# A chunked-attention and mixture-of-experts kernel: input loads in 2 KB runs four tiles ahead, v's loads tied to the next round's turns, and a routing table cleared in two steps

## The chip, the cores and the metric

The kernel runs on one core of a Trainium2 chip. The metric is the device time of one execution, in microseconds, lower is better. A profile of one execution shows what each engine did: PE (TensorE, matmuls), PEld (its weight loads), DVE (VectorE), ACT (ScalarE), POOL (GpSimd) and SP (SyncE, which here only issues DMAs). Sixteen DMA engines move all data between memory and the core, whoever issues the transfer.

## What is computed

Attention inside chunks of 64 tokens, then a mixture of experts that sends each token to one of eight experts:

```
# q, k, v: [8, 8, 576, 64] float32
scores = q_c @ k_c.T / 8 per chunk of 64;  attn = softmax(scores);  out = attn @ v_c
x = out.transpose(0, 2, 1, 3).reshape(4608, 512)
logits = x @ w_gate + modality_bias[modality_id]        # [4608, 8]
e_idx = argmax(logits);  gate_w = softmax(logits)[e_idx]
for e in range(8):                                      # w1[e]: 512x1024, w2[e]: 1024x512
    out[e_idx == e] = gate_w * (relu(x[e_idx == e] @ w1[e]) @ w2[e])
```

## The kernel before

The 4608 tokens are 36 tiles of 128. For each tile the attention stage does the following. `scores` (L248) multiplies q by k in 64 by 64 blocks, eight heads by two chunks; DVE takes the maximum and subtracts it (L250, L252); `exps` has ACT take the exponential (L257) and POOL add the two halves of each row (L258); `sums` has DVE finish the sum (L262). `transposes` (L269) turns the exponentials on PE and ACT copies them out (`at`, L271). `values` (L282) multiplies them by v, again in 64 by 64 blocks, and ACT copies the result out (`xt`, L285). `rows` (L294) multiplies with an identity beside the gate's weights, which gives the tile's rows and its logits; DVE scales them (`xr`, L296); `put` has ACT store the logits (L306) and issue the store of the rows to memory (`xd`, L307).

The order is written out by hand (`manual_schedule`) in rounds of four tiles (`ROUNDS`; the first three rounds have one, one and two tiles). A round k that begins with tile a has two halves. In the first half, the turns, PE does `transposes` of tiles a to a+3 and `rows` of the four tiles before. In the second half PE alternates `scores` of the next round's tiles with `values` of this round's. So 64 by 64 matmuls, with very many instructions for PE, fill the second half, and matmuls of the whole array the first. The PSUM tiles `ap` (of `transposes`) and `xp` (of `values`) share a ring of two buffers; ACT's copies `at` and `xt` free them.

The loads of q and k (`load_qk`, L116, 512 KB a tile, one tile `qk`) and of v (`load_v`, L122, 256 KB) are issued on SP's queue, which is in order; each waits until its buffer is free. Six buffers of each stand in a ring: behind `scores(t)` comes the load of q and k for tile t+6, behind `values(t)` the load of v for tile t+6.

Routing starts before attention is over. The tokens are routed in two groups, the first 14 tiles and the other 22 (`GROUPS`). `route` finds each token's expert and its row in a table in memory, `tab`, of 8 experts by 4608 rows of 64 bytes. `scatter` (L384) has POOL write one row for each token, an indirect DMA for each tile, 14 in the first group. Rows that no token took must hold an index out of bounds, so the table is cleared ahead: POOL fills a buffer with that value, and `clear_part` (L191) issues three DMAs of 768 KB on ACT's queue, one in round 5 and two in round 6 (`CLEARS`), each after the round's turns. After the first group, `locate` (L522) has SP read the first three slots' lists of tokens from the table (`tl`), POOL copies the indices (`tk`, L539), and `gather` (L543) has POOL fetch the rows of the slot's 384 tokens from `xd` into `xg`, in three indirect DMAs. `split` then turns these rows on PE (`tp`, L583), and the expert stage begins: 384 tokens a slot, for each of eight slices `first` (L640) and `second` (L653), every product in three passes of high and low parts. `fetch` (L600) has SP load the weights, and ACT and DVE split them (L611, L615).

What the program's builder orders by itself: DMAs issued from SP and ACT take turns on eight completion semaphores, DMAHW0 to DMAHW7, and POOL's indirect DMAs on eight others, DMASW0 to DMASW7. An access to `tab` whose rows are found at run time counts as one to the whole table; only the scatters are declared free of each other.

Of the kernel before, what the change touches and what calls it, by code (L numbers as in the profile page):

```python
# [8 lines left out]
F32 = mybir.dt.float32  # L9
# [10 lines left out]
P = 128  # L20
N = B * S
DM = H * D
E = 8
# [3 lines left out]
NT = N // P  # L27
NP = H // 2
SLOT = 384
# [5 lines left out]
BUSY = 4  # L35
SIZES = (1, 1, 2) + 8 * (4,)
ROUNDS = [(sum(SIZES[:i]), n) for i, n in enumerate(SIZES)]
CLEARS = (5, 6, 6)
PLAN = {
    -10: {"fetch": [(0, 1)]},  # L40
    -9: {"fetch": [(1, 1)]},
# [25 lines left out]
CAP = N  # L67
ROW = 16
# [4 lines left out]
NEG = 1  # L73
GMAX = max(n for _, n in GROUPS)
OFF = 16
EARLY = sum(n for _, n in GROUPS[:NEG])
# [18 lines left out]
def attention_moe(ctx: ExitStack, tc: tile.TileContext, qkv, mod, cst, bias, wcat, wfst, out):  # L95
    nc = tc.nc
    V, A, PE, G, SP = nc.vector, nc.scalar, nc.tensor, nc.gpsimd, nc.sync

    cp = ctx.enter_context(tc.tile_pool(name="cp", bufs=1))
    wk = ctx.enter_context(tc.tile_pool(name="wk", bufs=2))  # L100
# [6 lines left out]
    tab = dr.tile([E * CAP, ROW], I32, name="tab")  # L107


    NB = 6  # L110
    st = {}

    def load_qk(t):
        if t < NT:
            b = wk.tile([P, 2, DM], F32, name="qk", bufs=NB)
            SP.dma_start(b, qkv[t][:, 0:2])  # L116
            st[t] = {"qk": b}

    def load_v(t):
        if t < NT:  # L120
            b = wk.tile([P, DM], F32, name="v", bufs=NB)
            SP.dma_start(b, qkv[t][:, 2])  # L122
            st[t]["v"] = b

    cs = cp.tile([P, C_END], F32, name="cs")
# [5 lines left out]
    consts(C_I, C_GW)  # L131
    load_qk(1)
    load_v(0)
    load_qk(2)
    load_v(1)
    load_qk(3)
    load_v(2)
    load_qk(4)
    load_v(3)
    load_qk(5)  # L140
    load_v(4)
    load_v(5)
    bs = cp.tile([P, 2, E], F32, name="bs")
    mid = cp.tile([P, 2 * NT], I32, name="mid")

# [7 lines left out]
    ident = cs[:, C_I:C_I + P]  # L153
# [24 lines left out]
    tid = cp.tile([P, NT], I32, name="tid")  # L178
    G.iota(tid, pattern=[[P, NT]], base=0, channel_multiplier=1)
    oob = rawr[2].bitcast(I32)  # L180
    nclear = 3
    wclear = ROW * E * CAP // P // nclear
    oob = oob.rearrange("p a b -> p (a b)")[:, 0:wclear]
    G.memset(oob, OOB)
    tabp = tab.rearrange("(p a) c -> p (a c)", p=P)
    clears = []

    def clear_part():
        i = len(clears)
        if i < nclear:  # L190
            clears.append(A.dma_start(tabp[:, i * wclear:(i + 1) * wclear], oob))  # L191

    SYNC = mybir.DependencyInfo(mybir.DependencyClass.Sync, mybir.DependencyReason.DATA)

    def after(inst, names):
        for n in names:
            tc.add_manual_dep(inst.ins, n, SYNC, reason="rows of the token table")

    def apart(inst, key):
        tc.declare_no_dep(inst.ins, group=key, reason="scatters to different rows")  # L200
        tc.add_to_no_dep_group(key, inst.ins)
# [63 lines left out]
    def transposes(t):  # L265
        ex = st[t]["ex"].rearrange("p h k -> p (h k)")
        ap = ps.tile([P, NP, P], F32, tag="t", name="ap")
        for p in range(NP):
            PE.transpose(ap[:, p, :], ex[:, p * P:p * P + P], ident)  # L269
        at = mp.tile([P, DM], F32, tag="yo", name="at", bufs=4).rearrange("p (a c) -> p a c", a=NP)  # L270
        A.copy(at, ap)  # L271
        st[t]["at"] = at

    def values(t):
        v, at = st[t]["v"], st[t]["at"]
        xp = ps.tile([P, NP, P], F32, tag="t", name="xp")
        for p in range(NP):
            for c in range(2):
                vs = slice(p * P + c * 64, p * P + c * 64 + 64)
                for hh in range(2):  # L280
                    hs = slice(hh * 64, hh * 64 + 64)
                    PE.matmul(xp[hs, p, c * 64:c * 64 + 64], v[hs, vs],  # L282
                              at[hs, p, c * 64:c * 64 + 64], start=True, stop=True)
        xt = mp.tile([P, DM], F32R, tag="h", name="xt", bufs=6).bitcast(F32).rearrange("p (a c) -> p a c", a=NP)
        A.copy(xt, xp)  # L285
        st[t]["xt"] = xt
# [92 lines left out]
        pooljobs.append(scatter(g, pi, tg))  # L379

    def scatter(g, pi, tg):
        assert len(clears) == nclear
        for j in range(GROUPS[g][1]):
            w = G.indirect_dma_start(  # L384
                tab, bass.IndirectOffsetOnAxis(ap=pi[:, j:j + 1], axis=0),
                tg[:, j, :], None, bounds_check=E * CAP - 1, oob_is_err=True)
            after(w, [c.ins.name for c in clears])
            apart(w, "tab")
            marks.append(w.ins.name)
            yield  # L390
# [342 lines left out]
    scores(0)  # L733
    load_qk(NB)
    exps(0)
    late_consts()
    scores(1)
    load_qk(NB + 1)
    busy(BUSY)

    done, scored = 0, 2
    for k, (a, n) in enumerate(ROUNDS):
        whole = range(done, a) if k > 1 else ()
        for j in range(max(n, len(whole))):
            if j < n:
                transposes(a + j)
                if not k:
                    exps(1)
            if j < len(whole):
                rows(whole[j])  # L750
            if j < n:
                sums(a + j)
            if j < len(whole):
                put(whole[j])
                done = whole[j] + 1
                for g, (t0, m) in enumerate(GROUPS):
                    if t0 + m == done:
                        jobs.append(route(g))
            advance(None if j % 2 else [pooljobs])
        if k == 2:  # L760
            prepare()
        for _ in range(CLEARS.count(k)):
            clear_part()
        upto = a + 3 if k < 2 else a + n + ROUNDS[k + 1][1] if k + 1 < len(ROUNDS) else scored
        small = range(scored, upto)
        scored = upto
        for j in range(max(n, len(small))):
            if j < len(small):
                scores(small[j])
                load_qk(small[j] + NB)  # L770
            if j < n:
                values(a + j)
                load_v(a + j + NB)
            if j < len(small):
                exps(small[j])
            advance()
            if j < n:
                plan(a + j - NT)
# [26 lines left out]
def _pack(inputs):  # L805
    import numpy as np

    def chunks(a):
        return a.reshape(B, H, S // 64, 64, D).transpose(0, 2, 1, 3, 4).reshape(NT, 2, H, 64, D)

    q, k, v = (chunks(np.asarray(inputs[n])) for n in ("q", "k", "v"))
    qt = q.transpose(0, 1, 4, 2, 3).reshape(NT, 2, 64, DM)
    kt = k.transpose(0, 1, 4, 2, 3).reshape(NT, 2, 64, DM)
    vv = v.reshape(NT, 2, NP, 2, 64, D).transpose(0, 3, 4, 2, 1, 5).reshape(NT, 2, 64, DM)
    qkv = np.stack([qt, kt, vv], axis=3).reshape(NT, P, 3, DM)

    wg = np.asarray(inputs["moe_w_gate"])
    c = np.zeros((P, C_END), np.float32)
    gw = c[:, C_GW:C_GW + NP * GWC].reshape(P, NP, GWC)
    gw[:, :, 0:P] = np.eye(P, dtype=np.float32)[:, None, :]  # L820
    for hh in range(2):
        gw[hh * 64:(hh + 1) * 64, :, P + hh * E:P + (hh + 1) * E] = \
            wg.reshape(NP, 2, 64, E)[:, hh].transpose(1, 0, 2)
    c[:, C_GW:C_GW + NP * GWC] = gw.reshape(P, -1)
    c[:, C_I:C_I + P] = np.eye(P, dtype=np.float32)
    c[:, C_U:C_U + P] = np.triu(np.ones((P, P), np.float32), 1)
    c[:, C_REV:C_REV + E] = np.arange(E, 0, -1)
    c[:, C_CAP:C_CAP + E] = np.arange(E) * CAP
    c[:, C_EID:C_EID + E] = np.arange(E)
    c[:, C_DE:C_DE + 2 * E] = np.diff(np.arange(2 * E) % E, prepend=0)  # L830
    c[:, C_THR:C_THR + 3 * NJ] = (np.arange(NJ) * SLOT + np.arange(3)[:, None] * P).reshape(-1)
    c[:, C_LOW:C_LOW + 4 * E * E] = np.tril(np.ones((2 * E, 2 * E), np.float32), -1).reshape(-1)
    c[:, C_SID:C_SID + NREST] = np.arange(NREST)
    c[:, C_STP:C_STP + E], c[:, C_STP + E:C_STP + 2 * E] = SLOT, TAIL
    c[:, C_PEN + TAIL // P:C_PEN + NTT] = OOB
    c[:, C_TH2:C_TH2 + NJ2] = np.arange(NJ2) * TAIL

    w1 = np.asarray(inputs["moe_w1"]).reshape(E, NK, P, NF, P).transpose(0, 2, 3, 1, 4).reshape(E, P, NF, DM)
    w2 = np.asarray(inputs["moe_w2"]).reshape(E, NF, P, DM).transpose(0, 2, 1, 3)
    wcat = np.concatenate([w1, w2], axis=3)  # L840

    w1 = np.asarray(inputs["moe_w1"]).reshape(E, NK, NJB, 32, NF, P).transpose(0, 1, 3, 4, 2, 5).reshape(E, P, NF, DM)
    wfst = np.concatenate([w1, w2], axis=3)
    mod = np.ascontiguousarray(np.asarray(inputs["moe_modality_id"]).astype(np.int64).reshape(NT, P).T)
    bias = np.ascontiguousarray(np.broadcast_to(np.asarray(inputs["moe_modality_bias"])[None], (P, 2, E)))
    return {"qkv": qkv, "mod": mod, "cst": c, "bias": bias, "wcat": np.ascontiguousarray(wcat), "wfst": np.ascontiguousarray(wfst)}
# [18 lines left out]
```

## Time and profile before

| | |
|---|---|
| three runs | 566.11, 568.56, 568.07 us (median 568.07) |
| the profiled execution, its own time | 568.04 us |
| its span in the profile | 566.3 us |
| PE busy | 548.3 us (97%) |
| PE's weight loads, DVE, ACT, POOL busy | 499.3, 360.3, 248.0, 176.2 us |
| first 141 us (attention and routing): DMA share, rate | 0.90, 322 GB/s |
| the other 425 us (experts): DMA share, rate | 0.64, 207 GB/s |

In the timeline each row has the start in us, the busy time in us, the engine, the line, the operation, its tiles, how many instructions are merged in it, and in brackets the idle time ahead of it with what ended it; "issue" stands for an engine that waited for nothing that the profile shows. PE's matmuls in float32 stand as two records each, so a tile's `scores` have 32, and as many weight loads. In the table of stretches, the last three numbers are the clock that PE was granted, the busy share of the DMA engines, and the GB/s that they moved.

### The profile page before, as it was taken

How to read it: one execution, taken by the hardware profiler on the slowest of the kernel's cores; microseconds unless marked ns; L12 is line 12 of the kernel's file. 1: busy time of each engine (PE TensorE's matmuls, PEld its weight loads, DVE VectorE, ACT ScalarE, POOL GpSimd, SP SyncE). 2: the span in 40 equal slices, each digit the busy share in tenths (PEclk: the TensorE clock that was granted, in tenths of full speed). 3: DMA queues.
4: the chain of work that ended last, by engine and by line, in shares of the span. 5: the costliest groups of instructions: out<-in, count | busy, mean ns of one | idle time of the engine just before them, and what ended most of it. 6: DMA issues, size and time to landing. Idle time of an engine off the chain costs nothing.

```text
span 566.3 us, 12350 instructions
## 1 busy us (share of the span) xinstructions
PE 548.3 (97%) x4900; PEld 499.3 (88%) x4900; DVE 360.3 (64%) x633; ACT 248.0 (44%) x422; POOL 176.2 (31%) x182
## 2 busy tenths in 40 slices
PE   8989989999999999999999999999999999999994
PEld 6889979999889989989898999898898998989993
DVE  4767778886899665555656565565655646556741
ACT  3455544665434344443434434443434434444531
POOL 4322243742648753132230412213032210402001
PEclk9999989999999999999999999999999999999998
DMA  8998898879788748876683976748486673657410
GB/s 322 364 374 293 322 370 314 281 217 362 234 262 224 253 132 261 317 221 225 158 303 134 273 248 185 262 128 283 181 261 220 184 261 113 228 185 236 155 38 27
DMA packets 59538, 133.23 MB, mean 235 GB/s; under 512 B 11022, under 2 KB 29134, under 8 KB 53072
## 3 DMA queue, kind: packets, MB, share of 16 engines
q1 hardware_dynamic: 46064, 100.72, 53.7%
q0 software_dynamic: 7072, 19.18, 10.2%
q10 hardware_dynamic: 6336, 12.47, 5.9%
q8 instruction: 40, 0.66, 0.5%
q14 instruction: 26, 0.21, 0.1%
HBM read 102.16 MB, written 30.70 MB: 235 GB/s over the span
## 4 chain that ended last, share of the span: by engine, by line
PE 75%; issue 13%; DMA 3%; POOL 3%; DVE 2%; ACT 1%; ACTq 0%; POOLq 0%; DVEq 0%
PE yb L653 29%; PE hp L640 28%; PE sp L248 6%; PE xp L282 5%; PE yb L294 5%; PE ap L269 3%; DMA xg<-xd,tk 1%; POOL out L665 1%; DMA out<-yo,tk 1%; DMA xd<-xr 1%; PE yb L173 1%; POOL xg L543 1%; POOL lh L326 0%; DVE wl L615 0%; DVE ex L252 0%
## 5 line engine op out<-in xcount | busy, mean ns | idle before, releaser
L615 DVE TENSOR_TENSOR wl<-raw,wh 128x1024 fp32r<-128x1024 f32 (+1 forms) x106 | 129.5, 1223 | 36.4 <-ACT wh L611 36.0
L643 ACT ACTIVATE hh<-hp 128x384 fp32r<-128x384 f32 (+1 forms) x104 | 49.5, 476 | 217.4 <-PE hp L640 214.6
L640 PE MATMUL hp<-xl,wh 128*128 128x384 f32 (+1 forms) x416 | 136.4, 328 | 0.0
L640 PE MATMUL hp<-xh,wh 128*128 128x384 f32 (+1 forms) x416 | 136.2, 327 | 0.0
L640 PE MATMUL hp<-xh,wl 128*128 128x384 f32 (+1 forms) x416 | 136.1, 327 | 0.0
L644 DVE SCALAR_TENSOR_TENSOR hl<-hp,hh 128x384 fp32r<-128x384 f32 (+1 forms) x104 | 55.7, 536 | 111.2 <-ACT hh L643 111.1
L653 PE MATMUL yb<-wh,hl 128*128 128x512 f32 x296 | 117.3, 396 | 0.6 <-DVE hl L644 0.5
L653 PE MATMUL yb<-wh,hh 128*128 128x512 f32 x296 | 117.4, 397 | 0.0
L653 PE MATMUL yb<-wl,hh 128*128 128x512 f32 x296 | 116.7, 394 | 0.0
L665 POOL DMA_INDIRECT out<-yo,tk x37 | 46.9, 1266 | 222.9 <-DVE yo L664 215.3
L611 ACT CAST wh<-raw 128x1024 fp32r<-128x1024 f32 (+1 forms) x106 | 108.4, 1024 | 0.2 <-issue 0.2
L640 PEld LDWEIGHTS hp<-xl,wh 128*128 128x128 f32 x416 | 78.3, 188 | 4.0 <-DVE xl L585 0.2
L640 PEld LDWEIGHTS hp<-xh,wh 128*128 128x128 f32 x416 | 78.3, 188 | 3.9
L640 PEld LDWEIGHTS hp<-xh,wl 128*128 128x128 f32 x416 | 78.4, 188 | 0.0
L653 PEld LDWEIGHTS yb<-wh,hl 128*128 128x128 f32 x296 | 55.9, 189 | 15.0 <-DVE hl L644 1.5
L653 PEld LDWEIGHTS yb<-wl,hh 128*128 128x128 f32 x296 | 55.7, 188 | 9.6
L653 PEld LDWEIGHTS yb<-wh,hh 128*128 128x128 f32 x296 | 55.6, 188 | 9.0
L543 POOL DMA_INDIRECT xg<-xd,tk x37 | 40.8, 1101 | 26.1 <-PE tp L583 10.4
L384 POOL DMA_INDIRECT tab<-tg,pi x36 | 39.6, 1100 | 21.1 <-issue 8.6
L258 POOL TENSOR_TENSOR sr<-ex 128x256 f32<-128x256 f32 x36 | 26.2, 727 | 59.7 <-ACT ex L257 59.6
L282 PE MATMUL xp<-at,v 64*64 64x64 f32 x1152 | 40.6, 220 | 3.8 <-issue 3.7
L248 PE MATMUL sp<-qk 64*64 64x64 f32 x1152 | 41.5, 222 | 2.3 <-issue 2.1
(126 smaller groups left out, 532.7 us busy)
## 6 DMA issues: line engine op xcount, KB each, us to landing
raw<-in_wcat SPq DMA_DIRECT2D x48, 1024.0 KB, 6.1
qk<-in_qkv SPq DMA_DIRECT2D x36, 512.0 KB, 6.2
v<-in_qkv SPq DMA_DIRECT2D x36, 256.0 KB, 6.3
xd<-xr ACTq DMA_DIRECT2D x36, 256.0 KB, 3.7
xs<-xg SPq DMA_DIRECT2D x10, 768.0 KB, 4.2
xq<-xs SPq DMA_DIRECT2D x40, 192.0 KB, 3.6
tab<-raw ACTq DMA_DIRECT2D x3, 768.0 KB, 6.6
raw<-in_wfst SPq DMA_DIRECT2D x4, 512.0 KB, 5.4
```

The costliest lines, as they stand in the source:

```text
L248: PE.matmul(sp[cs_, h, :], b[cs_, 0, hs], b[cs_, 1, hs], start=True, stop=True)
L282: PE.matmul(xp[hs, p, c * 64:c * 64 + 64], v[hs, vs], at[hs, p, c * 64:c * 64 + 64], start=True, stop=True)
L294: PE.matmul(fp[:, p, 0:GWC], xt[:, p, :], gw[:, p, :], start=True, stop=True)
L384: w = G.indirect_dma_start(tab, bass.IndirectOffsetOnAxis(ap=pi[:, j:j + 1], axis=0), tg[:, j, :], None, bounds_check=E * CAP - 1, oob_is_ ...
L543: G.indirect_dma_start(xg[:, t, :], None, xd[0:n, :], bass.IndirectOffsetOnAxis(ap=tk[:, t:t + 1], axis=0), bounds_check=n - 1, oob_is_err ...
L611: A.copy(hi, raw)
L615: (G if pool else V).tensor_tensor(lo, raw, hi.bitcast(F32), ALU.subtract)
L640: PE.matmul(hp, a[:, ks], b[:, k, 0:n], start=(m == 0), stop=(m == 3 * NK - 1))
L643: A.activation(hh[:, 0:n], hp, AF.Relu)
L644: V.scalar_tensor_tensor(hl[:, 0:n], hp, 0.0, hh.bitcast(F32)[:, 0:n], ALU.max, ALU.subtract)
L653: PE.matmul(y, a[:, tsl], b[:, DM:2 * DM], start=(f == 0 and i == 0), stop=(f == NF - 1 and i == 2))
L665: w = G.indirect_dma_start(out, bass.IndirectOffsetOnAxis(ap=tk[:, t:t + 1], axis=0), yo, None, bounds_check=N - 1, oob_is_err=False)
```

## The change

The host stores each row of the input as q, v, k in place of q, k, v. A tile's q and k are then two runs of 2 KB in each partition, where they were one of 4 KB. The ring of q and k has four buffers in place of six: behind `scores(t)` comes the load for tile t+4. The ring of v keeps six, but v's loads move: from round 3 on, the load of v for tile t+2 stands behind the `transposes` of tile t, and a manual dependency makes it wait for the last of them. So a round's four loads of v come with its turns, and its four loads of q and k with its second half.

The table is cleared by four DMAs, one each in rounds 5, 6, 8 and 9. The first two clear, for each expert, the rows that the first group's tokens and the first three slots can reach (2176 of 4608 rows; 557 KB a DMA), the last two the others (623 KB a DMA). The scatters of the first group are told to wait for the first two alone.

```
-CLEARS = (5, 6, 6)
+CLEARS = (5, 6, 8, 9)
...
-    NB = 6
+    NB, NV = 4, 6
...
-            SP.dma_start(b, qkv[t][:, 0:2])
+            SP.dma_start(b, qkv[t][:, 0:3:2])
...
-    def load_v(t):
+    def load_v(t, hold=None):
...
+            d = SP.dma_start(b, qkv[t][:, 1])
+            if hold is not None:
+                after(d, [hold.ins.name], "loads of v while the whole array works")
...
+        a, n = (0, low_rows) if i < 2 else (low_rows, CAP - low_rows)
+        e0, m = i % 2 * (E // 2), ROW * n // P
+        clears.append(A.dma_start(
+            tabe[e0:e0 + E // 2, ROW * a:ROW * (a + n)].rearrange("e (p m) -> p e m", p=P),
+            oob[:, 0:m].unsqueeze(1).to_broadcast([P, E // 2, m])))
...
+        cleared = clears[:2] if g < NEG else clears
...
-                transposes(a + j)
+                hold = transposes(a + j)
+                if k > 2:
+                    load_v(a + j + 2, hold)
...
-                load_v(a + j + NB)
+                if k < 2:
+                    load_v(a + j + 4)
...
-    qkv = np.stack([qt, kt, vv], axis=3).reshape(NT, P, 3, DM)
+    qkv = np.stack([qt, vv, kt], axis=3).reshape(NT, P, 3, DM)
```

On SP's queue, in the middle of the attention stage, before (`qk` is the tile of q and k, `v` that of v):

```order
L122 DMA v<-in_qkv 128x512
L116 DMA qk<-in_qkv 128x1024
L122 DMA v<-in_qkv 128x512
L116 DMA qk<-in_qkv 128x1024 x3
L122 DMA v<-in_qkv 128x512
L116 DMA qk<-in_qkv 128x1024
```

The same place on SP's queue now, where a row holds four loads:

```order
L116 DMA qk<-in_qkv 128x2x512 x4
L122 DMA v<-in_qkv 128x512 x4
L116 DMA qk<-in_qkv 128x2x512 x4
L122 DMA v<-in_qkv 128x512 x4
L116 DMA qk<-in_qkv 128x2x512 x4
L122 DMA v<-in_qkv 128x512 x4
```

Loads that alternated now stand in blocks of four.

On ACT's queue, at the end of round 8's turns, before, with the semaphores that each instruction waits for:

```order
L307 DMA xd<-xr 128x512 [waits DMAHW6_49]
L271 COPY at<-ap 128x512 [waits PE_49,Activation_49]
L306 COPY lp_140<-yb_104 128x64 [waits DVE_49]
L307 DMA xd<-xr 128x512 [waits DMAHW7_49]
L285 COPY xt<-xp 128x512 [waits PE_49]
L257 ACTIVATE ex<-ex 128x512 [waits DVE_49,Pool_49]
```

The same place on ACT's queue now:

```order
L309 DMA xd<-xr 128x512 [waits DMAHW3_49]
L272 COPY at<-ap 128x512 [waits PE_49,Activation_49]
L308 COPY lp_132<-yb_96 128x64 [waits DVE_49]
L309 DMA xd<-xr 128x512 [waits DMAHW4_49]
L190 DMA tab<-raw_107 128x4x304 [waits DMAHW6_49,DMASW0_49]
L287 COPY xt<-xp 128x512 [waits PE_49]
```

The third clear stands between the last store of the turns and the first copy `xt` of the round. It waits for DMASW0, the semaphore of the first group's first and ninth scatters; in the built program the wait is for the second of the two landings. The fourth clear stands at the same place of round 9 and waits in the same way for DMASW5, at the landing of the fourteenth scatter.

On POOL's queue, the first group's ninth scatter and those after it, now:

```order
L387 DMA tab<-tg_125,pi_1648 36864x16 [waits DMASW0_49]
L259 TENSOR_TENSOR sr_134<-ex 128x8x32 [waits Activation_49]
L387 DMA tab<-tg_125,pi_1648 36864x16 [waits DMAHW6_49,DMASW1_49]
L259 TENSOR_TENSOR sr_135<-ex 128x8x32 [waits Activation_49]
L387 DMA tab<-tg_125,pi_1648 36864x16 [waits DMASW2_49]
L259 TENSOR_TENSOR sr_136<-ex 128x8x32 [waits Activation_49]
```

The order is as before, but the tenth scatter now waits for DMAHW6 too, the third clear's semaphore. SP's read of the first list, `tl`, waits in the same way for the third and the fourth clear.

More of the change, by code (lines that the diff above doesn't have):

```diff
@@ L115, in load_qk @@
             b = wk.tile([P, 2, DM], F32, name="qk", bufs=NB)
-            SP.dma_start(b, qkv[t][:, 0:2])
+            SP.dma_start(b, qkv[t][:, 0:3:2])
             st[t] = {"qk": b}
-    def load_v(t):
+    def load_v(t, hold=None):
         if t < NT:
-            b = wk.tile([P, DM], F32, name="v", bufs=NB)
-            SP.dma_start(b, qkv[t][:, 2])
+            b = wk.tile([P, DM], F32, name="v", bufs=NV)
+            d = SP.dma_start(b, qkv[t][:, 1])
+            if hold is not None:
+                after(d, [hold.ins.name], "loads of v while the whole array works")
             st[t]["v"] = b
@@ L137, in attention_moe @@
     load_v(2)
-    load_qk(4)
     load_v(3)
-    load_qk(5)
-    load_v(4)
-    load_v(5)
     bs = cp.tile([P, 2, E], F32, name="bs")
@@ L180, in attention_moe @@
     oob = rawr[2].bitcast(I32)
-    nclear = 3
-    wclear = ROW * E * CAP // P // nclear
-    oob = oob.rearrange("p a b -> p (a b)")[:, 0:wclear]
+    low_rows = EARLY * P + SLOT
+    oob = oob.rearrange("p a b -> p (a b)")[:, 0:ROW * (CAP - low_rows) // P]
     G.memset(oob, OOB)
-    tabp = tab.rearrange("(p a) c -> p (a c)", p=P)
+    tabe = tab.rearrange("(e r) c -> e (r c)", e=E)
     clears = []
@@ L189, in clear_part, with after @@
         i = len(clears)
-        if i < nclear:
-            clears.append(A.dma_start(tabp[:, i * wclear:(i + 1) * wclear], oob))
+        a, n = (0, low_rows) if i < 2 else (low_rows, CAP - low_rows)
[3 more added lines that the diff above has]
+            oob[:, 0:m].unsqueeze(1).to_broadcast([P, E // 2, m])))
     SYNC = mybir.DependencyInfo(mybir.DependencyClass.Sync, mybir.DependencyReason.DATA)
-    def after(inst, names):
+    def after(inst, names, reason="rows of the token table"):
         for n in names:
-            tc.add_manual_dep(inst.ins, n, SYNC, reason="rows of the token table")
+            tc.add_manual_dep(inst.ins, n, SYNC, reason=reason)
     def apart(inst, key):
@@ L268, in transposes @@
         for p in range(NP):
-            PE.transpose(ap[:, p, :], ex[:, p * P:p * P + P], ident)
+            hold = PE.transpose(ap[:, p, :], ex[:, p * P:p * P + P], ident)
         at = mp.tile([P, DM], F32, tag="yo", name="at", bufs=4).rearrange("p (a c) -> p a c", a=NP)
@@ L272, in transposes @@
         st[t]["at"] = at
+        return hold
     def values(t):
@@ L381, in scatter @@
     def scatter(g, pi, tg):
-        assert len(clears) == nclear
+        cleared = clears[:2] if g < NEG else clears
+        assert len(cleared) == (2 if g < NEG else 4)
         for j in range(GROUPS[g][1]):
@@ L386, in scatter @@
                 tg[:, j, :], None, bounds_check=E * CAP - 1, oob_is_err=True)
-            after(w, [c.ins.name for c in clears])
+            after(w, [c.ins.name for c in cleared])
             apart(w, "tab")
```

## The prediction

> **What bounds the kernel now.** I read the page first: PE is busy nearly all the time, at full clock but in one place, and the DMA engines are crowded in the first quarter, the attention stage.
>
> ```profile
> span 566.3 us, 12350 instructions
> PE 548.3 (97%) x4900; PEld 499.3 (88%) x4900; DVE 360.3 (64%) x633; ACT 248.0 (44%) x422; POOL 176.2 (31%) x182
> ...
> q8 instruction: 40, 0.66, 0.5%
> ```
>
> So only PE's own waits can be won. The list of PE's waits, cut to the first 141 us, has these:
>
> ```profile
> PE xp L282 <- issue: 3.7, 2, 2.5
> PE sp L248 <- issue: 2.1, 2, 1.5
> ```
>
> With a third, of 0.44 at `rows`, the waits on "issue" sum to 6.2 us. No row there waits for qk or v. PE's timeline shows where the five stalls stand:
>
> ```profile
> 22.23 0.73 PE L282 MATMUL xp<-at,v 64*64 64x64 f32 x17 [1.15 <-issue]
> ...
> 35.10 0.85 PE L248 MATMUL sp<-qk 64*64 64x64 f32 x21 [1.50 <-issue]
> ...
> 51.70 0.50 PE L248 MATMUL sp<-qk 64*64 64x64 f32 x9 [0.62 <-issue]
> ...
> 78.96 0.63 PE L282 MATMUL xp<-at,v 64*64 64x64 f32 x15
> 82.11 1.12 PE L282 MATMUL xp<-at,v 64*64 64x64 f32 x17 [2.52 <-issue]
> ...
> 113.12 0.77 PE L294 MATMUL yb<-cs,xt 128*128 128x144 f32 x5 [0.44 <-issue]
> ```
>
> Each falls inside a tile, whose operands had all been there (15 of 32 matmuls done, then 2.52 us of nothing, then 17). Counted through PE's program (64 records and weight loads for a tile's `scores` or `values`, 24 for a turn with its `rows`), the five stand 504, 760, 1266 and 1268 instructions apart: two, three, five and five times about 253. So PE runs out of instructions at regular borders, and only at some. The page's queue of instructions moves 0.66 MB in 40 packets, 16 KB each: the next piece of program comes by DMA and is late where the DMA engines are full. The table of stretches bears it out:
>
> ```profile
> 58.00:60.00 2.00, 2.00 (x45) 1.85 (x45) 1.81 (x5) 0.98 (x4) 0.00 (x0) 1.00 0.63 246
> ...
> 78.00:80.00 2.00, 1.59 (x55) 1.46 (x50) 1.86 (x6) 1.21 (x2) 0.39 (x1) 1.00 1.04 424
> 80.00:82.00 2.00, 0.00 (x0) 0.00 (x0) 1.93 (x6) 0.01 (x1) 0.72 (x1) 0.90 1.00 402
> 82.00:84.00 2.00, 1.89 (x21) 1.77 (x21) 0.49 (x3) 0.72 (x2) 0.00 (x0) 0.50 1.02 411
> 84.00:86.00 2.00, 2.00 (x15) 2.00 (x14) 0.28 (x1) 0.96 (x2) 0.72 (x1) 0.74 1.07 424
> ```
>
> The longest stall lies in a share of 1.0; four borders between the third and the fourth stall passed unseen, two of them, by the count, at 60 to 64 us, behind the quiet stretch at 0.63. After that stall the clock was granted at 0.90, 0.50 and 0.74: 1.72 us of clock lost, 0.2 of it inside the stall, so 1.5 us paid.
>
> **The loads, part by part.** The chain of waits gives a pair of `scores` and `values` 0.93 + 0.93 us, and a turn with its `rows` 0.44 + 0.98; the DMA table gives each load's size and landing:
>
> ```profile
> 77.26 0.93 PE xp L282 x32
> 78.20 0.93 PE sp L248 x32
> ...
> 87.11 0.44 PE ap L269 x4
> 87.54 0.98 PE yb L294 x8
> ```
>
> ```profile
> qk<-in_qkv SPq DMA_DIRECT2D x36, 512.0 KB, 6.2
> v<-in_qkv SPq DMA_DIRECT2D x36, 256.0 KB, 6.3
> xd<-xr ACTq DMA_DIRECT2D x36, 256.0 KB, 3.7
> xs<-xg SPq DMA_DIRECT2D x10, 768.0 KB, 4.2
> ...
> tab<-raw ACTq DMA_DIRECT2D x3, 768.0 KB, 6.6
> ...
> tl<-tab SPq DMA_DIRECT2D x13, 3.0 KB, 3.3
> ```
>
> Before, a pair asks for 768 KB in 1.86 us, 423 GB/s, against the 402 to 424 that a full share moved: saturated, and round 6 adds 1.5 MB of clears. After, it asks for 512 KB, 282 GB/s, and a round's one clear of 557 KB adds 75 over the four pairs. The turns carry v's 256 KB and the stored 256 KB: in 1.42 us, so 369 GB/s, near full, but there PE takes 1.42 us for 24 instructions, not 1.86 for 128, and has long to wait for the next piece. So the stalls should mostly go. What may stay is a border just behind the turns; I leave 1.3 us for such and take a gain of 6.2 + 1.5 - 1.3 = **6.4 us**, between 4.5 (a stall of half the longest remains, with its clock) and 7.7 (all).
>
> Runs of 2 KB instead of 4: v's loads have them already and land in 6.3 us, q and k's in 6.2, so no price; at the worst a tenth of a microsecond at the start, where the first tile is waited for. Four tiles ahead: q and k are now asked for a round ahead, 4 x (1.86 + 1.42) = 13.1 us, against a landing of 6.2. v's load for the third tile of a round stands behind the first turn's transposes, 0.98 + 3 x 1.42 + 2 x 1.86 + 0.93 = 9.9 us ahead of use, against 6.3. So I cost both at nothing; if the cover went, PE would wait at `sp` or `xp` for a DMA by what a landing is over these.
>
> **The clears.** This is where the change adds waits. The third clear is on ACT, in order, and waits for the ninth scatter to land; behind it stand the copies `xt` and the exponentials of the round. PE's third `values` of the round needs a PSUM buffer that the first `xt` frees. The rows of before for that place, POOL, ACT and PE:
>
> ```profile
> 73.64 1.14 ACTq L191 DMA_DIRECT2D tab<-raw  x2
> ...
> 106.17 0.59 ACT L285 COPY xt<-xp 128x512 f32<-128x512 f32 x1 [0.85 <-PE xp L282]
> ...
> 118.98 0.33 ACTq L307 DMA_DIRECT2D xd<-xr  x1
> ...
> 106.74 0.98 POOL L384 DMA_INDIRECT tab<-tg,pi  x1 [0.30 <-issue]
> ...
> 109.24 0.99 POOL L384 DMA_INDIRECT tab<-tg,pi  x1 [0.16 <-issue]
> ...
> 116.61 0.98 POOL L384 DMA_INDIRECT tab<-tg,pi  x1 [0.30 <-issue]
> ...
> 108.75 1.10 PE L282 MATMUL xp<-at,v 64*64 64x64 f32 x32
> ...
> 122.80 1.10 PE L282 MATMUL xp<-at,v 64*64 64x64 f32 x32
> ```
>
> The tile view of `tab` gives the landing of scatters one by one: a quiet one at 104.2, the ninth itself at 106.7, a crowded one at 111.5.
>
> ```profile
> DMA to landing us min/median/max: 2.6/2.6/2.6
> DMA to landing us min/median/max: 4.8/4.8/4.8
> DMA to landing us min/median/max: 5.4/5.4/5.4
> ```
>
> The times below are on before's clock; the gain only shifts them. I take 4.0 us for the ninth scatter, since the loads beside it are thinner: landed at 110.74. Then 0.57 for the issue (1.14 for two), 0.59 for `xt`, some 0.15 for signals (an estimate, the gap between a copy and its reader in such rows): PE goes on at 112.05, not 108.75: **3.3 us** (1.9 at 2.6, 4.7 at 5.4).
>
> The tenth scatter waits for the clear to land. A clear of 768 KB took 6.6 us in the full share, a store of 768 KB 4.2 elsewhere, 256 KB 3.7; for 623 KB in a quiet moment I take 4.0: 114.74 instead of 109.24. POOL's sums queue behind it, but DVE wants them one by one in the turns that follow, so the turns of round 9 hide it; past them, each us that POOL is late would hold a turn. The fourteenth comes 7.37 us later (109.24 to 116.61), 122.1, and lands at 125.1, with 3.0 us in a moment without loads. ACT reaches the fourth clear at 118.98 + 0.33 + 3.3 = 122.6, waits till then, and frees PE at 126.4; PE, shifted, wants it at 122.80 + 3.3 = 126.1: **0.3 us** (0 to 5.3, if every landing is of the crowded kind).
>
> The read of the lists waits for the fourth clear, at 125.1 + 4.0 = 129.1. Before:
>
> ```profile
> 121.61 2.75 SPq L522 DMA_DIRECT2D tl<-tab  x3
> ...
> 125.95 0.19 POOL L539 COPY tk<-tl 128x3 int32<-128x3 int32 x1
> ...
> 137.86 0.33 PE L583 MATMUL tp<-cs,xg 128*128 128x128 f32 x1 [0.94 <-DMA xg<-xd,tk]
> ```
>
> Shifted by 3.6 us the read would have been at 125.2, so it is 3.9 late; about 1.1 of that was slack ahead of `tk` (a landing of 3.3 after 121.61 is 124.9, the copy began at 125.95). Behind it on SP stand v's last two loads and the weights, which move with it. The gathers come 2.8 us late into the same traffic, and PE already waited 0.94 us for the last of them, so there is no cover: I take **2.0 us** (1.3 to 4.6), as the stores to `xd` will be further along then.
>
> Two idle times of about 3 us now stand on PE. The one of 2.52 cost 1.5 us of clock, those of 1.15 and 1.50 nothing; I take **1.8 us** for both (0.5 to 3.0). [...]
>
> **The sum** against the profiled execution's own 568.04 us (1.7 us over its span, and at the median of the runs, 568.07): -6.4 + 3.3 + 0.3 + 2.0 + 1.8 = +1.0, so **569.0 us**. About 0.5%, 2.8 us, is what a measurement of this kernel can tell from no change, so this is a forecast of no change: two effects of a size that nearly cancel, 565.2 to 570.9.
>
> **The rivals.**
>
> *The new waits cost more (slower).* Scatter landing of 4.8 us, its own row, and clears of 5.3, between 4.0 and 6.6: PE held 4.1 us at the first; the fourth clear issued after 128, 2.6 us more; the lists 5.2 late, 3.3 at `tp`; 2.5 of clock. 12.5 - 6.4 = +6.1, 574.1 us. It decides once the waits cost 9.2 us. For it: in a trace where the DMA engines are full the scatters landed in 4.8 to 5.4. Against: after the change the second half of a round is thinner. Chance 0.25.
>
> *The waits are short (faster).* Landings of 2.6 and 3.7: 1.9 at the third clear, none at the fourth, 1.3 at `tp`, 0.5 of clock, 3.7 in all, with the full gain of 7.7: 564.0 us. For it: the quiet scatter did land in 2.6. Chance 0.27.
>
> *The stalls are not the loads' doing (slower).* Then nothing is won and the waits cost 7.4: 575.4 us. [...] The rows at a share of 1.0 and of 0.63 speak against this rival. Chance 0.05.
>
> **How the numbers follow.** No change 0.43; faster 0.27; slower 0.25 + 0.05 = 0.30. The range reaches from 562.5, a little under the faster case, to 577, over both slower ones; the corner in which every landing is crowded (about 580) is left out.
>
> **What would show it.** PE's "issue" waits under 2 us and none of 2.5 at the round with the clears: the first step. A wait of POOL's scatter or of `xt` on the clears' landing, and PE idle some 3 us before an `xp` of round 8: the second. `tl` issued 7 us or so later against the turns of round 10, and PE's wait at `tp` grown from 0.94 to about 3: the third. Wrong would be: PE waits for qk or v; stalls of the old size at the borders; or no idle at round 8, if the clears find their scatters landed already.

## The result and the profile after

The changed kernel takes 578.11 us (median of 4 runs, 576.27 to 578.85); the kernel before, beside it on the same chip, 568.17 us (4 runs, 566.11 to 568.56). The ratio is 1.0166 [1.0132, 1.0200]: slower, by about 9.4 us. The profiled execution's span is 577.1 us, against 566.3. Here and in the experiments, executions far above the fastest of their kernel are left out of the ratio, though not of the median beside it: e1 has one of 1094 us and e2 one of 1594, so that e2's ratio rests on three.

PE's waits now, in the first 155 us (us in total, times, longest):

```profile
PE xp L284 <- ACT xt L287: 6.2, 2, 3.5
PE xp L284 <- issue: 3.5, 2, 2.9
PE sp L249 <- issue: 2.3, 2, 1.4
PE tp L586 <- DMA xg<-xd,tk: 2.1, 1, 2.1
...
PE sp L249 <- DMA qk<-in_qkv: 0.6, 2, 0.5
```

Two things are to be seen. A wait of 6.2 us for ScalarE's `xt` is new. And the waits on "issue", which were to go, are there: 3.5 + 2.3 = 5.8 us, against 6.2. PE's timeline shows the places:

```profile
33.80 0.85 PE L249 MATMUL sp<-qk 64*64 64x64 f32 x21 [1.43 <-issue]
...
50.67 0.50 PE L249 MATMUL sp<-qk 64*64 64x64 f32 x9 [0.89 <-issue]
...
78.30 0.63 PE L284 MATMUL xp<-at,v 64*64 64x64 f32 x15
81.87 0.68 PE L284 MATMUL xp<-at,v 64*64 64x64 f32 x17 [2.94 <-issue]
...
96.68 0.34 PE L284 MATMUL xp<-at,v 64*64 64x64 f32 x5 [0.59 <-issue]
...
113.03 1.34 PE L284 MATMUL xp<-at,v 64*64 64x64 f32 x32 [3.50 <-ACT xt L287]
...
130.96 1.97 PE L284 MATMUL xp<-at,v 64*64 64x64 f32 x32 [2.73 <-ACT xt L287]
...
148.69 0.33 PE L586 MATMUL tp<-cs,xg 128*128 128x128 f32 x1 [2.08 <-DMA xg<-xd,tk]
```

The stalls at 34, 51 and 82 us stand at the very matmuls of before (21, 9 and 17 left of 32), and the longest has grown from 2.52 to 2.94 us. The one at 22 us is gone, and a small one at 97 us is new. The two new waits stand before the third `values` of rounds 8 and 9. ACT's timeline says who holds them:

```profile
105.57 0.33 ACTq L309 DMA_DIRECT2D xd<-xr  x1
111.95 0.40 ACTq L190 DMA_DIRECT2D tab<-raw  x1
112.39 0.59 ACT L287 COPY xt<-xp 128x512 f32<-128x512 f32 x1 [6.61 <-DMA tab<-tg,pi]
...
129.88 0.40 ACTq L190 DMA_DIRECT2D tab<-raw  x1
130.32 0.59 ACT L287 COPY xt<-xp 128x512 f32<-128x512 f32 x1 [5.87 <-DMA tab<-tg,pi]
```

ACT stands idle from the store at 105.57 to the clear at 111.95 (6.61 us before the copy), and 5.87 us again at the fourth clear: it waits for a scatter, and the copy `xt` stands behind the clear. POOL's rows close the loop, first the ninth scatter, then the tenth, which waits for the clear, the fourteenth, and the cast of the first lists:

```profile
106.87 0.98 POOL L387 DMA_INDIRECT tab<-tg,pi  x1 [0.30 <-issue]
...
119.11 0.99 POOL L387 DMA_INDIRECT tab<-tg,pi  x1 [4.80 <-DMA tab<-raw]
...
126.19 0.98 POOL L387 DMA_INDIRECT tab<-tg,pi  x1 [0.30 <-issue]
...
135.59 0.19 POOL L542 COPY tk<-tl 128x3 int32<-128x3 int32 x1
```

The table of stretches (PEclk, DMA share and GB/s are the last three columns) shows what follows the first of the two waits, and how full the engines were at the stall of round 6:

```profile
112.00:114.00 2.00, 0.97 (x30) 0.97 (x32) 0.00 (x0) 1.61 (x4) 0.41 (x1) 0.96 1.06 360
114.00:116.00 2.00, 2.00 (x44) 2.00 (x42) 0.00 (x0) 1.52 (x3) 0.31 (x1) 0.50 0.97 361
116.00:118.00 2.00, 2.00 (x38) 1.93 (x35) 1.38 (x2) 0.36 (x1) 0.00 (x0) 0.69 0.57 171
...
76.00:80.00 4.00, 2.93 (x102) 2.84 (x97) 3.76 (x12) 2.33 (x5) 1.44 (x3) 1.00 1.06 380
```

After the first wait the clock is halved, which costs 2 x (0.04 + 0.50 + 0.31) = 1.7 us. The same follows the second wait (0.72, 0.50 and 0.92 in the stretches from 130 to 136 us), and the stall of round 6 as before (0.53 and 0.62 from 83 to 87 us).

The sum: 6.2 (waits for `xt`) + 3.4 (two more halvings) + 1.1 (`tp`, 2.08 in place of 0.94) + 0.6 (`sp` for q and k) - 0.4 (issue) = 10.9 us, against 577.1 - 566.3 = 10.8 between the spans.

### The profile page after: what moved, and what is told of

The parts are those of the page before. It is cut to its first block, busy times and chain, and to the rows that moved or that the text cites. A ratio compares the mean times of both kernels' runs of the same rounds, so it can differ in the third digit from the quotient of the medians.

```text
span 577.1 us, 12357 instructions
## 1 busy us (share of the span) xinstructions
PE 551.4 (96%) x4899; PEld 502.2 (87%) x4900; DVE 360.7 (63%) x633; ACT 247.5 (43%) x422; POOL 172.2 (30%) x182
## 4 chain that ended last, share of the span: by engine, by line
PE 68%; issue 14%; DMA 7%; POOL 5%; DVE 3%; ACT 1%; POOLq 0%; ACTq 0%; DVEq 0%
PE yb L656 28%; PE hp L643 28%; PE yb L296 4%; PE sp L249 4%; PE xp L284 3%; POOL tab L387 2%; PE ap L270 2%; DMA tab<-tg,pi 2%; DMA xg<-xd,tk 1%; DMA cs<-in_cst 1%; DMA tab<-raw 1%; POOL sr L259 1%; POOL out L668 1%; DMA raw<-in_wcat 1%; DMA qk<-in_qkv 1%
## 5 line engine op out<-in xcount | busy, mean ns | idle before, releaser
L284 PE MATMUL xp<-at,v 64*64 64x64 f32 x1152 | 42.1, 224 | 9.9 <-ACT xt L287 6.2
L284 PEld LDWEIGHTS xp<-at,v 64*64 64x64 f32 x1152 | 38.7, 140 | 10.9 <-ACT xt L287 6.5
```

Of the source, the lines that this page charges most:

```text
L284: PE.matmul(xp[hs, p, c * 64:c * 64 + 64], v[hs, vs], at[hs, p, c * 64:c * 64 + 64], start=True, stop=True)
```

## The experiments

Theory W: the waits of the two late clears cost all of it, and the rest of the change costs nothing. Theory F: the issue stalls are pieces of the instruction stream that come late behind other DMA traffic. A border is the place where one piece of that stream, 16 KB by the page's 40 packets of 0.66 MB in all, ends and the next begins. The rivals stand in the expectations. The runs fell on four chips. On the two of e1 to e4 and of e13 and e14 the kernel before took 567.6 and 568.5 us; on those of e5, e6, e7 and e9, and of e8 and e10 to e12, it took 578.8 and 576.9, with runs 2% apart, so there a profile tells more than a ratio. Each ratio is to before on the same chip.

**e1, the changed kernel with its clears early.**

```
-CLEARS = (5, 6, 8, 9)
+CLEARS = (5, 5, 6, 6)
```

> The changed kernel with its four clears all issued in rounds 5 and 6, ahead of every scatter, so that no clear waits for a scatter and no scatter for a later clear. Theory W (the new waits of the third and fourth clear cost the time: 6.2 us at PE's values, two more halvings of the clock, 1.5 us each, and 1.2 us more at the turn of the gathered rows, 10.4 in all): 566 to 569 us, no wait of a copy on a scatter, no wait of values on that copy. Rival L (the loads in 2 KB runs, or their new order, cost the time): 574 us or more.

570.55 us, 1.0044 [1.0014, 1.0075]. No wait of ACT for a scatter and none of PE for `xt` is left. Of the 1.66% only 0.44% remains. The time is above theory W's 566 to 569 us and far under rival L's 574: theory W holds for the larger part, and something else costs the rest.

**e2, the kernel before with the new clears alone.**

```
-CLEARS = (5, 6, 6)
+CLEARS = (5, 6, 8, 9)
...
+        a, n = (0, low_rows) if i < 2 else (low_rows, CAP - low_rows)
...
+        cleared = clears[:2] if g < NEG else clears
```

> The kernel before with nothing changed but the clears: four, in two steps, in rounds 5, 6, 8 and 9. Theory W: 576 to 580 us, with copies that wait about 6 us for a scatter twice. Rival L: 566 to 570 us.

579.58 us, 1.0187 [1.0155, 1.0220], from three executions. PE's waits in this profile:

```profile
PE xp L285 <- ACT xt L288: 5.0, 2, 4.1
PE xp L285 <- issue: 3.5, 2, 2.2
PE tp L587 <- DMA xg<-xd,tk: 2.9, 1, 2.9
PE sp L251 <- issue: 2.6, 2, 2.3
```

The clears by themselves make the whole loss, with the loads as they were.

**e3, the kernel before with q, v, k stored in the new order.**

```
-    qkv = np.stack([qt, kt, vv], axis=3).reshape(NT, P, 3, DM)
+    qkv = np.stack([qt, vv, kt], axis=3).reshape(NT, P, 3, DM)
```

(and the two loads' slices with it)

> The kernel before with q, v, k as the order in memory, so that q and k are two runs of 2 KB; loads, order and clears as before. Theory W: 567 to 570 us, within 0.4% of before, with the stalls at the borders of the program still there. Rival L, by the runs: 572 us or more, since the packets of q and k moved 20.5 GB/s an engine in the changed kernel against 22.8 before.

569.67 us, 1.0045 [1.0023, 1.0068]. A small loss, just over the 0.4% that theory W allowed. The stalls did not shrink in sum (2.6 + 2.2 + 1.8 = 6.6 us in its profile), but stand partly elsewhere.

**e4, the changed kernel's order and depth of loads, with runs of 4 KB and the old clears.**

```
-    NB = 6
+    NB, NV = 4, 6
...
+                hold = transposes(a + j)
+                if k > 2:
+                    load_v(a + j + 2, hold)
```

> The changed kernel's order and depth of loads, with q, k, v as the order in memory (one run of 4 KB) and the three clears of before. Theory W: 562 to 569 us. If the stalls at the borders come from the loads' crowding and the 2 KB runs kept the crowd, they shrink here to 3 us in all and the time is 563 to 565; if they come from the clears and stores on the other queue, the one of round 6 stays at 2.5 us or more. Rival L, by the order: 572 us or more.

568.22 us, 1.0007 [0.9986, 1.0027]: the new order is worth nothing by itself. Its profile has stalls of 3.1 + 2.7 + 0.3 us, with one of 2.80 in round 6. That was expected if the clears and stores make it; e14 has such a stall without a clear.

**e5, the changed kernel without the false waits.** The rows of the late clears and of the first group's scatters do not overlap, but their addresses are known only at run time, so the builder makes each wait for the other. Here they are declared free of each other.

```
+        if i > 1:
+            apart(clears[-1], "high")
+            apart(clears[-1], "read")
...
+            if g < NEG:
+                apart(w, "high")
...
+        if s < NEARLY:
+            apart(rd, "read")
```

> The changed kernel, with the third and fourth clear where they stand (before rounds 8 and 9), but declared free of the scatters of the first group and of the first three list reads, whose rows they do not touch; the second group's scatters still wait for them. Nothing is left out. Theory W (the waits of the clears are what the change costs): the two waits of TensorE at values L284 for ScalarE's xt, 6.2 us in the changed kernel, fall under 0.5 us, the wait at tp L586 for the gather (2.1 us) goes back to about 1 us, and the time comes to 578.1 - 6.2 - 1.1 = about 571, near the 570.6 measured with the clears put early. Rival C (the clears' 1.2 MB of traffic at this place delays loads, scatters and row writes, whether they wait or not): the waits go but others come in their place, and the time stays at 575 or above.

580.11 us where before took 578.76: 1.0032 [0.9994, 1.0070]. ACT no longer waits for a scatter, and PE's wait for `xt` is down to 0.5 us, with the clears at their places. This speaks for the wait and against the clears' traffic at this point (rival C), but does not settle it: the changed kernel did not run on this chip, and on the chip of e12, which is about as slow, PE waited only 1.1 us for `xt`. The 2.7 us at `tp` did not go back to about 1 as expected.

**e6, 30 small matmuls more at the start of the kernel before.**

```
+    for i in range(SMALL):
+        PE.matmul(yb[1][:, 1, 0:16], warm[:, 0:P], warm[:, 0:16], start=True, stop=True)
```

> The kernel before, with 30 more warming matmuls (16 columns each) on TensorE right behind the eight that are there, before the first tile has landed; nothing is left out. Theory B (the waits named issue come when TensorE has used up a piece of its instruction stream of fixed length, about 126.6 matmul records, and the next piece is not there yet): every border stands 30 matmuls earlier in the program. The wait of round 6, which in the kernel before splits the last values of that round into 15 and 17 matmuls, splits the scores ahead of it into 17 and 15, at 1.5 to 3 us; the one at 22 us splits scores 17 and 15 instead of values 15 and 17; their sum stays within 3 to 9 us. The time stays within 1% of before, since the 30 matmuls (some 2 us) end before the first loads. Rival (the waits belong to something at these places of the program, such as a tile of v that is late and that the trace does not name): they stay at the same matmul of the same group.

582.38 us, 1.0029 [0.9992, 1.0067]. PE's timeline in round 6, and around 35 us:

```profile
81.76 0.74 PE L251 MATMUL sp<-qk 64*64 64x64 f32 x18
85.33 0.62 PE L251 MATMUL sp<-qk 64*64 64x64 f32 x13 [2.83 <-issue]
...
35.61 0.74 PE L285 MATMUL xp<-at,v 64*64 64x64 f32 x19 [2.25 <-issue]
```

Before, the stall of round 6 left 17 matmuls of the last `values` to do. Now it leaves 13 of the `scores` ahead of it (the row lacks one record), and the stall at 35 us leaves 19 of a `values` in place of 21 of the next `scores`: both stand 30 matmuls earlier in the program (28 by the first count). The wait belongs to a count of instructions, not to a tile or its data. Counted from PE's first one in the profile, the stall of round 6 stands behind 3222 or 3223 matmuls and weight loads in before, in the changed kernel and in every run but e9 (3236); in e6, 60 of them are the new ones. The stall that was to move at 22 us is not there in this run, and there are others at borders, at 27 and 71 us; the four sum to 7.8 us (3 to 9 were expected). The border decides where a stall can be. That the traffic decides whether it is, this run does not show; e9 and e8 bear on it.

**e7, the kernel before with one clear in the middle of the turns of rounds 4, 5 and 6.**

```
-CLEARS = (5, 6, 6)
+CLEARS = (4, 5, 6)
...
+            if j == 1 and k in CLEARS:
+                clear_part()
```

> The kernel before, with its three clears issued one each in rounds 4, 5 and 6, in the middle of the turns, instead of one ahead of round 5's scores and two ahead of round 6's; nothing is left out. Theory F (a piece of the instruction stream comes late when it is asked for while the 16 DMA engines are full, with the clears' packets of 9.8 KB among those ahead of it): the 2.5 us wait of round 6, whose piece was asked for at 75.8 us and started at 79.9 us with the clears in the queues, falls under 1 us, the halved clock behind it (1.5 us) goes, and the time is 564 to 566. Rival D (loads fill the engines by themselves, whatever the clears do): the wait stays at 1.5 to 3 us, in round 6 or another, and the time is 567 to 570.

577.34 us, 0.9992 [0.9954, 1.0029]. The stall of round 6 fell to 1.31 us, between the two forecasts (under 1, and 1.5 to 3), and the clock stayed whole behind it (1.00 from 50 to 105 us). Round 6 has one clear here in place of two, and at another place, so the run cannot tell number from place. The gain that theory F expected is not seen at this spread. (The clears' packets are of 6 KB, not of 9.8 KB as the expectation has it.)

**e8, the kernel before, cleared in two steps, the late clears where nothing is waited for.**

```
-CLEARS = (5, 6, 6)
+CLEARS = (4, 5, 10, 10)
```

(with the new clears of e2)

> The kernel before with the table cleared in the changed kernel's two steps, but at other places: the two clears of what the first lists reach before the scores of rounds 4 and 5, the two of the rest together before round 10, where the scatters that they wait for have long landed. Nothing is left out, and round 6 has no clear. Theory F (the issue wait of 2.5 us in round 6 is a piece of the instruction stream that comes behind the clears' packets): the wait in round 6 falls under 1 us, TensorE waits for xt less than 0.5 us in all, and the time against before falls by 0.2 to 0.8%, unless the late clears delay the gathers of the first lists: then the wait at tp L583 grows from 0.9 us to 3 or more and the gain is lost. Rival D (loads alone fill the engines): the wait of round 6 stays at 1.5 to 3 us and the time is that of before, within 0.3%.

577.68 us, 1.0011 [0.9966, 1.0056]. PE's timeline has a stall of only 0.22 us in round 6, and this in round 4:

```profile
53.24 0.58 PE L251 MATMUL sp<-qk 64*64 64x64 f32 x9 [2.81 <-issue]
```

At this border, with 9 left, before stood 0.62 us. The long stall has gone with the clear from round 6 to round 4, into a share of 1.02 (52 to 54 us), and the clock fell to 0.50 behind it (54 to 56 us). The gain of 0.2 to 0.8% that theory F expected is not seen, and PE waited 1.0 us for `xt`, where less than 0.5 was expected.

**e9, the kernel before without v's loads from the seventh tile on** (the first six v are used again, so the later results are those of other values).

```
+        if NB <= t < NT:
+            st[t]["v"] = vs[t % NB]
```

> The kernel before without its loads of v from the seventh tile on: the v of the first six tiles is used again instead, so the attention's results from there on are those of other values. This takes 13 MB of the loads away, a third of what q, k and v bring. Theory F (the issue waits are late pieces of the instruction stream, late because the 16 DMA engines are full): with the engines no longer full the waits from 30 us on fall from 4.9 us to under 1.5 us in all, no clock halving follows, and the time is 558 to 564 (563 from those stalls alone, less where loads or row writes were in the way too). Rival S (the pieces are late for a reason that the DMA load does not set): the issue waits stay at 4 us or more, and the time at 566 to 569.

572.67 us, 0.9925 [0.9869, 0.9981]. The loads that are left out carry 7.9 of 28.3 MB, 28%, and not the 13 MB of the expectation. Between 30 and 76 us, where before has 1.50 and 0.62 (and e7, on this chip, 1.71, 0.62 and 0.65), no stall of over 0.5 us is left; the DMA share from 20 to 50 us is 0.84 at 292 GB/s, where before has 0.94 at 350. But in round 6, with two clears, one remains:

```profile
78.53 0.50 PE L286 MATMUL xp<-at,v 64*64 64x64 f32 x10 [2.54 <-issue]
```

So theory F's number (under 1.5 us in all) was missed: taking away 28% of these loads ends the small stalls, and the long one stays in the round with two clears. By the number alone rival S would have it (4 us or more), for the issue waits of the first 150 us sum to 5.4; but 2.5 of them, around 100 us, and those around 200 us are of a kind told of at the end. The ratio agrees with theory F's upper end.

**e10 and e11, the clears in runs of 2 KB,** at the old places, and in the turns as in e7.

```
-    tabp = tab.rearrange("(p a) c -> p (a c)", p=P)
+    tabp = tab.rearrange("(a p r) c -> p a (r c)", a=3 * nclear, p=P)
```

> The kernel before with its three clears at their places, written as runs of 2 KB instead of 6 KB; nothing is left out. Theory P (a piece of the instruction stream waits on its DMA engine for the packets that stand ahead of it, one or more of each queue, so the clears' packets of 240 ns each lengthen the wait most): with packets of some 90 ns the 2.5 us wait of round 6 falls to 1.5 us or under, and the time by 0.1 to 0.5%. Rival T (what counts is the bytes ahead, or the share): the wait stays at 2 us or more, and the time within 0.2% of before.

> The kernel before with its three clears in runs of 2 KB and one each in the middle of the turns of rounds 4, 5 and 6; nothing is left out. If both the size of the packets and the place count, the issue waits of rounds 4 to 6 fall under 1 us in all, no halved clock follows in that stretch, and the time is 0.4 to 0.8% under before. If neither counts, the time is within 0.2% of before.

579.33 us, 1.0031 [0.9978, 1.0083], and 577.49 us, 1.0010 [0.9969, 1.0052]. The stall of round 6 is 2.75 us in e10 and 1.11 in e11 (1.31 in e7, with longer runs): the number and place of the clears count, the size of their packets does not. Theory P falls. (At 80 us in before, a clear's packet of 6 KB took 219 ns on average and one of 2 KB 84 ns, where the expectation has 240 and 90.) In e11 another stall, of 1.44 us, stands in round 4, so the sum for rounds 4 to 6 is not under 1 as was expected. The times tell nothing at this spread.

**e12, the changed kernel once more, on the chip of e8, e10 and e11.**

> The changed kernel unchanged, on the chip of the three others. Theory W: TensorE waits for xt by 5 to 7 us in all, and the ratio to before is 1.012 to 1.020 here too. If the ratio is under 1.008, the loss hangs on the chip and not on the waits alone.

581.53 us, 1.0098 [1.0057, 1.0140]: between the bounds that were set (1.012 and 1.008). Theory W's 5 to 7 us of wait for `xt` did not come; the profile has 1.1:

```profile
105.04 0.25 PE L249 MATMUL sp<-qk 64*64 64x64 f32 x1 [1.11 <-issue]
...
105.75 0.21 PE L284 MATMUL xp<-at,v 64*64 64x64 f32 x1 [0.40 <-issue]
106.50 1.73 PE L284 MATMUL xp<-at,v 64*64 64x64 f32 x29 [0.54 <-issue]
...
127.10 1.15 PE L284 MATMUL xp<-at,v 64*64 64x64 f32 x32 [1.09 <-ACT xt L287]
```

On this chip PE halts at matmul after matmul around 105 us. Meanwhile the ninth scatter (issued at 104.43 us) lands and the clear goes out at 107.39, so the first of the two waits is hidden. By this one profile, the size of the loss hangs on what else holds PE.

**e13 and e14, no late clear that waits and none in rounds 4 and 6:** e13 on the kernel before (with the new clears), e14 on the changed one.

```
+CLEARS = (5, 5, 10, 10)
```

> The kernel before, cleared in two steps: both clears of what the first lists reach before the scores of round 5, both of the rest before round 10. Nothing is left out. Theory F (a long issue wait stands where a border of the instruction stream falls in the scores and values of a round that has a clear: rounds 4 and 6 have such a border, round 5 has not): no wait of over 1 us in rounds 4 to 6 (51 to 95 us), against 0.6 + 2.5 before; TensorE waits about 1 us for xt at round 10, where the issue of two clears holds ScalarE. On a chip on which before runs at 566 to 570 us, the time is 0.3 to 0.7% under it. Rival D (loads alone fill the engines, and a wait of 2 us or more comes at some border anyhow): one wait of over 2 us in these rounds, and the time within 0.2% of before.

> The changed kernel with both of its first clears before round 5 and both of the rest before round 10. Nothing is left out. Theories W and F together: TensorE's waits for xt fall from 6.2 us to about 1, the 2.9 us issue wait of round 6 goes, and the time is 0 to 0.4% over before (what the 2 KB runs cost, 0.45% when they stood alone, less what the wait of round 6 cost). Rival D: the wait of round 6 stays at 2 us or more, and the time is 0.4 to 0.8% over before.

e13: 565.82 us where before took 568.45, 0.9968 [0.9946, 0.9990]. e14: 567.35 us, 0.9977 [0.9956, 0.9999]. Round 6 in e13, PE's timeline and then the stretches:

```profile
81.01 0.69 PE L285 MATMUL xp<-at,v 64*64 64x64 f32 x17 [1.38 <-issue]
```

```profile
76.00:80.00 4.00, 3.63 (x125) 3.49 (x120) 3.74 (x11) 2.57 (x5) 1.19 (x2) 1.00 1.03 400
80.00:82.00 2.00, 0.99 (x20) 0.92 (x20) 1.92 (x6) 0.30 (x2) 0.72 (x1) 1.00 0.97 383
82.00:84.00 2.00, 2.00 (x19) 2.00 (x18) 1.22 (x5) 1.33 (x3) 0.73 (x1) 1.00 1.05 415
```

and in e14:

```profile
79.63 0.69 PE L284 MATMUL xp<-at,v 64*64 64x64 f32 x17 [2.36 <-issue]
```

```profile
76.00:80.00 4.00, 1.64 (x56) 1.56 (x54) 3.73 (x13) 1.19 (x2) 0.74 (x2) 1.00 0.94 315
80.00:82.00 2.00, 2.00 (x22) 1.93 (x18) 0.07 (x1) 1.59 (x3) 0.44 (x1) 0.69 0.39 133
82.00:84.00 2.00, 2.00 (x11) 1.99 (x11) 1.10 (x3) 0.21 (x1) 0.29 (x1) 0.50 0.40 123
```

With before's loads the stall falls from 2.52 to 1.38 us (at most 1 was expected), the clock stays whole, and the kernel is faster than before and than the changed kernel. With the changed loads the stall is 2.36 us, with its halved clock, in a round that has no clear at all: for e14 the rival's stall came, and its time did not (0.23% under before, where 0.4 to 0.8% over was expected by it, and 0 to 0.4% over by theories W and F). PE's wait for `xt` fell to 1.1 us, as theory W has it.

These two kernels differ in the loads alone, and ran on one chip. The new loads, for which the prediction took a gain of 6.4 us, bring none here: the mean of e14's twelve executions is 567.1 us, that of e13's 566.2, a difference of 0.9 with some 1 us either way.

## Why the prediction was wrong, point by point

**The step that failed: "So the stalls should mostly go", a gain of 6.4 us.** The issue waits fell by 0.4 us, and the halving of 1.7 us behind the longest stayed. With the clears out of the way the new loads gained nothing either (e13 against e14; e4). Two of the prediction's own signs of being wrong came: stalls of the old size at the borders, and PE waiting for `qk`. That PE runs dry at borders of its instruction stream was right (e6), and the runs bear out that the piece is late where the DMA engines are full (e9; in e8 the stall moved with the clear). What was wrong is that the new order of loads thins the traffic where it counts. It set a demand of 282 + 75 = 357 GB/s against the 402 to 424 that before moved at a full share. But that rate belongs to the mix of before's round 6, at and behind the stall. What counts for the late piece is the stretch from the crossing of the border ahead of the stall (found by counting 253 instructions back) to the start of the piece's packet. It is, in before, the changed kernel, e14 and e13:

```profile
75.70:79.90 4.20, 3.89 (x133) 3.76 (x130) 3.96 (x11) 2.74 (x6) 1.45 (x2) 1.00 0.94 370
75.10:79.60 4.50, 3.83 (x131) 3.74 (x128) 4.23 (x13) 2.81 (x6) 1.63 (x3) 1.00 1.00 358
73.40:77.30 3.90, 3.87 (x127) 3.79 (x126) 3.66 (x11) 2.30 (x5) 1.46 (x2) 1.00 1.03 352
75.70:78.60 2.90, 2.90 (x108) 2.90 (x104) 2.75 (x7) 1.72 (x4) 1.45 (x2) 1.00 1.00 374
```

The engines were full in all four, in the changed kernel at 358 GB/s: 357 was no thin traffic but all that they moved there. In each of the four PE went on 2.2 to 2.4 us after the piece's packet began, so the stalls of 2.52, 2.94, 2.36 and 1.38 us follow the delays of 4.2, 4.5, 3.9 and 2.9. The share alone does not set the delay, since it is near 1 in e13 too. The long rows of 20 to 50 us show full engines at a lower rate with no clear at all, before and after:

```profile
20.00:50.00 30.00, 27.10 (x640) 25.98 (x638) 21.57 (x43) 16.05 (x32) 8.29 (x13) 1.00 0.94 350
```

```profile
20.00:50.00 30.00, 28.16 (x676) 27.04 (x671) 22.75 (x44) 17.26 (x34) 9.11 (x13) 1.00 0.93 313
```

37 GB/s less was moved at nearly the same share. e4 has 0.89 at 303 there with runs of 4 KB, e3 0.97 at 354 with runs of 2 KB, near before: it goes with the order and depth of the loads, not with the run's length. Why each byte keeps an engine longer in that order, no run shows.

**2 KB runs at no price.** Alone they cost 0.45% [0.23, 0.68] (e3), about 2.6 us, where a tenth of a microsecond was the worst foreseen. Whether e14 pays it cannot be told from the 0.9 us, with 1 us either way, that it lies over e13; the cause stays open.

**Four tiles ahead at nothing:** nearly right. PE waited 0.6 us for q and k, and e4's ratio is 1.0007 [0.9986, 1.0027].

**The third clear: 3.3 us** (1.9 to 4.7). It was 3.50, with the right mechanism and some luck in the size. The ninth scatter took 5.1 us to land, where 4.0 was taken, near the crowded row; by the prediction's sum that makes 4.4. PE came to this place 0.8 us later than in before (109.53 against 108.75), which made up for most of it. From the end of `xt` to PE's next matmul it took 0.05 us (112.98 to 113.03), where 0.15 was taken.

**The fourth clear: 0.3 us** (0 to 5.3). It cost 2.73: a mis-sized term. The third clear landed at about 119.0, 7.1 us after its issue and not 4.0; the share was still 1.06 to 0.97 when it went out. So the tenth scatter went at 119.11, the fourteenth at 126.19, and that one took 3.7 us to land (3.0 were taken).

**The lists: 2.0 us** (1.3 to 4.6) at `tp`. It was 1.1, under the range: the read went at 133.32, later than the 129.1 foreseen, but PE was late by the waits ahead of it too.

**The clock: 1.8 us** (0.5 to 3.0) for both waits. It was 3.4, over the range: the clock was halved behind both, 1.7 us each. That was not bound to come from their length alone, for behind stalls of 2.83 us in e6 and 2.75 us in e10 it stayed whole (1.00 from 50 to 105 us).

So the waits cost 3.50 + 2.73 + 1.1 + 3.4 = 10.7 us in place of 7.4, between that and the 12.5 of the slower rival, and nothing paid for them. With no gain it is the rival "The stalls are not the loads' doing", but not in its reason, for the loads do make stalls, as e9 shows, and not in its sum of 575.4, which had the waits at 7.4. The time came near the corner that the range left out (about 580), but by another way: that corner had every landing crowded and the gain of 6.4, while no case of the prediction put dearer waits and no gain together.

## What to carry to other kernels

The lower demand of the new loads was no gain here, for their transfers still filled the DMA engines (a share of 1.00 in the changed kernel, 1.03 in e14); with 28% of the loads left out, at 0.84, the small stalls went (e9). So compare a demand with the rate that the same mix of transfers reaches at a full share (358 GB/s here), not with the highest rate in the trace (424). The late clears, put between scatters and reads of the same tensor, took on their waits, though no byte is shared, and what stood behind them on ACT, in order, waited too (6.61 and 5.87 us): put such a transfer where what it waits for has long landed (e13), or tell the builder that the rows are apart (e5). When a wait is made of a chain of landings, price each at the crowded row as long as the share beside it is near 1: the ninth scatter and the third clear landed after 5.1 and 7.1 us here, where 4.0 was taken for each.

## What the hardware showed

- An instruction border can be moved: 30 more matmuls at the start moved two stalls 30 and 28 matmuls up the program (e6). The packets of the instruction queue show how late a piece can be: in before, the piece after the border crossed at about 60.0 us began 0.4 us later (share 0.05), that after the one at 75.7 us 4.2 us later (share 0.94).
- The same idle time does not always cost the clock. These rows of e2 and of e3 stand behind 2.21 us each. In e2 the 17 matmuls took 1.12 us, as in before at a clock of 0.50, and the second `transposes` behind them began 3.58 us after the first of them (86.83 us); in e3 they took 0.68 us, and it was 2.09 us (84.20):

```profile
83.25 1.12 PE L285 MATMUL xp<-at,v 64*64 64x64 f32 x17 [2.21 <-issue]
```

```profile
82.11 0.68 PE L282 MATMUL xp<-at,v 64*64 64x64 f32 x17 [2.21 <-issue]
```

Behind 2.36 us in e14 the clock fell too (0.69 and 0.50 from 80 to 84 us); behind 2.54 in e9, 2.75 in e10 and 2.83 in e6 it did not (1.00 from 76 to 82 us in e9, from 50 to 105 us in e10 and e6). What decides it, no run here shows.

- On two of the four chips PE showed single matmuls 0.4 to 1.2 us apart between 100 and 112 us in each kernel profiled there, at no border, and again near 200 us, up to 2.5 us apart, in all but one; and the kernel before was 1.5 to 2% slower than on the others. What makes them, no run here shows.
